# The reciprocal of softmax row sums, moved from VectorE to Newton steps on GpSimd

## The chip, the cores and the metric

The kernel runs on one core of a Trainium2 chip. The metric is the device time of one execution, in microseconds (us); lower is better. A core has five engines that work side by side: TensorE (PE in the profile) for matrix products, VectorE (DVE), ScalarE (ACT), GpSimd (POOL), and SyncE (SP), which here issues DMA transfers. Each engine runs its own instructions in program order. Where one needs the result of another, it waits on a semaphore.

## The reference: what is computed

Top-k attention with 8 batches, 8 heads, 576 positions and 64 values per head, then a feed-forward block on the 4608 rows of 512 values that it gives. All data is float32.

```python
scores = scale * np.matmul(q, k.transpose(0, 1, 3, 2))
kth = np.partition(scores, -top_k, axis=-1)[..., -top_k:-top_k + 1]   # top_k = 32
scores = np.where(scores >= kth, scores, -1000000000.0)
scores = scores - np.max(scores, axis=-1, keepdims=True)
attn = np.exp(scores)
attn = attn / (np.sum(attn, axis=-1, keepdims=True) + 1e-09)
x = np.matmul(attn, v)            # then heads side by side: 4608 x 512
h = x @ w_in                      # 512 -> 2048
g = h * np.cos(h)
out = g @ w_out                   # 2048 -> 512
```

The division in the sixth line is what the change concerns.

## The kernel before

The work is cut into 144 units. A unit is 128 query rows of one pair of heads, so most of its tiles have a middle dimension of 2. The main loop takes one slot per unit, and in a slot several units are in different stages: `u` searches its top 32, `w` (one slot older) is masked and exponentiated, `x` (two older) is normalised and its probabilities are split into 16-bit halves, `y` (three older) is transposed by a DMA, and `z` is a pair of units that are multiplied with the values. Pieces of the feed-forward block are put between.

VectorE searches: four rounds, each with a MAX8 and, but for the last, a MATCH_REPLACE8 for each of the two heads.

```python
def topk_round(u, rnd):
    ...
    for j in range(2):
        nc.vector.max(m8[:, j, at], src[:, j])                       # L237
    if rnd < TOPK // 8 - 1:
        for j in range(2):
            nc.vector.match_replace(rest[:, j], m8[:, j, at], src[:, j], NEG)   # L240
```

ScalarE masks and exponentiates, and sums each row as it does so. Then VectorE takes the reciprocal of the two sums of a row, and GpSimd multiplies:

```python
def exponentials(u):
    ...
    for j in range(2):
        nc.scalar.activation(out=s[:, j], in_=s[:, j], func=AF.Exp, bias=nd[:, j : j + 1],
                             scale=1.0, accum_out=den[:, j : j + 1])             # L268
    nc.scalar.activation(out=den, in_=den, func=AF.Identity, bias=eps, scale=1.0)  # L273

def reciprocal(u):
    u["rden"] = small.tile([P, 2], F32, tag="rden", name="rden")
    nc.vector.reciprocal(u["rden"], u.pop("den"))                                # L277

def normalise(u):
    s, rden = u["s"], u.pop("rden")
    for j in range(2):
        nc.gpsimd.tensor_scalar(out=s[:, j], in0=s[:, j], scalar1=rden[:, j : j + 1],
                                scalar2=1.0, op0=ALU.mult, op1=ALU.mult)         # L282

def split(u):
    ...
    halves = work.tile([P, 2, 2 * S], U16, tag="halves", name="halves", bufs=1)
    nc.gpsimd.tensor_copy(out=halves, in_=s.rearrange("p (k h) -> p h k", h=2))  # L294
```

`write_halves` then sends the halves to DRAM (`rows`), and `transposes` reads them back with a transposing DMA into `pT`, which TensorE multiplies with the values (L343).

GpSimd also works for the feed-forward block. For each tile `g` of 128 x 1024 hidden values it brings the argument of the cosine into range with four instructions (`reduce_first`, `reduce_second`), and after ScalarE's sine it multiplies (`gate`):

```python
gp.tensor_scalar(out=x, in0=g, scalar1=1.0, scalar2=0.25, op0=ALU.mult, op1=ALU.add)     # L431
gp.tensor_scalar(out=x, in0=x, scalar1=1.0, scalar2=MAGIC, op0=ALU.mult, op1=ALU.add)    # L432
gp.tensor_scalar(out=x, in0=x, scalar1=-MAGIC, scalar2=1.0, op0=ALU.add, op1=ALU.mult)   # L433
...
nc.gpsimd.tensor_tensor(out=x, in0=g, in1=x, op=ALU.subtract)                            # L440
...
eng.tensor_tensor(out=g, in0=g, in1=x, op=ALU.mult)                                      # L457, gate
```

Earlier still, while the weights arrive as 64-bit words, GpSimd has two more instructions for each weight piece (L147, L148). That is over after some 125 us.

The order of one slot of the main stage, cut to what matters (the other engines' calls stand between and run beside):

```python
def slot(i, u, w, x, y, z):
    if x: reciprocal(x)
    if u: topk_round(u, 0); ...
    if w: bounds(w); mask(w); exponentials(w)
    if u: topk_round(u, 1); topk_round(u, 2); topk_round(u, 3)
    ...                         # values(z), scores and take_scores of the next unit
    if y: transposes(y)
    gate(1)
    if x: normalise(x); split(x); write_halves(x)
    ...                         # feed-forward pieces
    reduce_first()
    reduce_second()
    ...
```

The first nine slots (`early_slot`) and the slots from the 142nd on (`last_slot`) transpose on TensorE instead (`transposes_now`). There the row sums, the reciprocal, the normalisation and the transposes of the same unit follow each other within one slot.

Of the kernel before, what the change touches and what calls it, by code (L numbers as in the profile page):

```python
# [10 lines left out]
F32 = mybir.dt.float32  # L11
I32 = mybir.dt.int32
U32 = mybir.dt.uint32
U16 = mybir.dt.uint16
AF = mybir.ActivationFunctionType
ALU = mybir.AluOpType

P = 128
# [7 lines left out]
INV_2PI = 1.0 / (2.0 * math.pi)  # L26
TWO_PI_BELOW = 6.283185005187988
MAGIC = 1.5 * 2.0**23


@with_exitstack
def kernel(
# [9 lines left out]
    nc = tc.nc  # L42
# [13 lines left out]
    consts = ctx.enter_context(tc.tile_pool(name="consts", bufs=1))  # L56
    loads = ctx.enter_context(tc.tile_pool(name="loads", bufs=5))
    work = ctx.enter_context(tc.tile_pool(name="work", bufs=2))
    small = ctx.enter_context(tc.tile_pool(name="small", bufs=4))
# [7 lines left out]
    nc.vector.memset(halfpi, math.pi / 2.0)  # L67
    eps = consts.tile([P, 1], F32, tag="eps")
    nc.vector.memset(eps, EPS)

# [191 lines left out]
    def exponentials(u):  # L264
        s, nd = u["s"], u.pop("nd")
        den = u["den"] = small.tile([P, 2], F32, tag="den", name="den")
        for j in range(2):
            nc.scalar.activation(  # L268
                out=s[:, j], in_=s[:, j], func=AF.Exp, bias=nd[:, j : j + 1], scale=1.0,
                accum_out=den[:, j : j + 1],  # L270
            )

        nc.scalar.activation(out=den, in_=den, func=AF.Identity, bias=eps, scale=1.0)  # L273

    def reciprocal(u):
        u["rden"] = small.tile([P, 2], F32, tag="rden", name="rden")
        nc.vector.reciprocal(u["rden"], u.pop("den"))  # L277

    def normalise(u):
        s, rden = u["s"], u.pop("rden")  # L280
        for j in range(2):
            nc.gpsimd.tensor_scalar(  # L282
                out=s[:, j], in0=s[:, j], scalar1=rden[:, j : j + 1], scalar2=1.0,
                op0=ALU.mult, op1=ALU.mult,
            )

# [127 lines left out]
    def reduce_first():  # L414
# [6 lines left out]
        if ff["end"]:  # L421

            nc.vector.tensor_scalar(
                out=x, in0=g, scalar1=0.25, scalar2=MAGIC, op0=ALU.add, op1=ALU.add
            )
            nc.vector.scalar_tensor_tensor(
                out=x, in0=x, scalar=MAGIC, in1=g, op0=ALU.subtract, op1=ALU.subtract
            )
            return
        gp = nc.gpsimd  # L430
# [4 lines that stand above are left out]
# [105 lines left out]
    def early_slot(i, u, w):  # L540
# [7 lines left out]
        if w:  # L548
            bounds(w)
            mask(w)  # L550
            exponentials(w)
            reciprocal(w)
# [5 lines left out]
        if w:  # L558
            normalise(w)
# [19 lines left out]
    def slot(i, u, w, x, y, z):  # L579
        if x:  # L580
            reciprocal(x)
# [3 lines left out]
        if w:  # L585
            bounds(w)
            mask(w)
            exponentials(w)
# [19 lines left out]
        if x:  # L608
            normalise(x)
            split(x)  # L610
            write_halves(x)
# [9 lines left out]
    def last_slot(i, u, w, x, y, z):  # L621
        if x:
            reciprocal(x)
# [3 lines left out]
        bounds(w)  # L627
        mask(w)
        exponentials(w)
        take_banks()  # L630
        sines(1)
# [10 lines left out]
        if x:  # L642
            normalise(x)
            split(x)
            write_halves(x)
# [25 lines left out]
    for i in range(NU + 1):  # L671
# [4 lines left out]
        u, w = (units[i - n] if 0 <= i - n < NU else None for n in range(2))  # L676
# [55 lines left out]
```

## Time and profile before

| | |
|---|---|
| median of three runs | 1535.46 us (1535.19 to 1535.78) |
| span of the profiled execution | 1530.3 us |
| reciprocal on VectorE (L277), 144 times | 22.9 us busy, 159 ns mean |
| VectorE waiting for the row sums before it | 17.4 us in 6 cases |
| GpSimd waiting for the reciprocal | 84.4 us in 29 cases |
| GpSimd waiting for the halves' DMA | 80.1 us in 42 cases |

A page of the profile is read from the top: the share of the span that each engine is busy, then the chain of work that ended last, followed back from the last instruction, then the costliest groups of instructions. A group's line names the source line, the engine, the operation, the tile written and the tiles read, the shapes and the count; after the first bar stand its busy time in us and the mean duration of one in ns, after the second the idle time of the engine just before these instructions and what ended most of it. Idle time of an engine that is not the bound costs nothing by itself, but it is the room in which that engine can take more work.

### The profile page before, as it was taken

The page shows a single profiled execution, that of the slowest core. Times are in us where ns is not written, and L with a number is a line of the kernel's source. Part 1 is how long each engine was busy: PE and PEld are TensorE (multiplying, and loading weights), DVE is VectorE, ACT ScalarE, POOL GpSimd, SP SyncE. Part 2 cuts the span into 40 slices and gives each one's busy share as a digit, 9 for nine tenths or more (in the row PEclk, how much of TensorE's full clock was granted, in tenths as well). Part 3 has the DMA queues.
Part 4 walks back from the last instruction along what each step waited for, and adds up shares of the span by engine and source line. Part 5 has one row for each costly group of instructions (what it writes and reads, how often), then busy time and mean ns, then how long its engine had stood idle before and what let it go on. Part 6 is the DMA issues. An engine that isn't in the chain of part 4 may idle for free.

```text
span 1530.3 us, 28322 instructions
## 1 busy us (share of the span) xinstructions
PE 1430.3 (93%) x10360; PEld 1022.7 (67%) x10360; DVE 1449.0 (95%) x3102; ACT 1109.6 (73%) x2150; POOL 1105.4 (72%) x838
## 2 busy tenths in 40 slices
PE   4678588999999999999999999999999999999998
PEld 3466266676767676767676767676767676767675
DVE  7999999999999999999999999999999999999911
ACT  7887667777777777777777777777777777777731
POOL 4778957777878787877777777777777778777600
PEclk6588899999999999999999999999999999999999
DMA  8432255645674556655565365645654446444200
GB/s 269 139 96 90 87 152 151 177 116 162 163 178 116 147 133 169 170 132 146 162 170 140 117 162 162 163 131 137 187 148 142 135 131 162 144 136 120 81 8 14
DMA packets 371740, 212.09 MB, mean 139 GB/s; under 512 B 321296, under 2 KB 337937, under 8 KB 371601
## 3 DMA queue, kind: packets, MB, share of 16 engines
q1 hardware_dynamic: 366192, 200.63, 48.4%
q10 hardware_dynamic: 5408, 9.65, 1.7%
q8 instruction: 81, 1.33, 0.4%
q14 instruction: 59, 0.48, 0.1%
HBM read 45.09 MB, written 87.29 MB: 87 GB/s over the span
## 4 chain that ended last, share of the span: by engine, by line
DVE 72%; PE 16%; ACT 5%; issue 5%; DMA 1%; POOL 0%; SPq 0%; ACTq 0%; POOLq 0%; DVEq 0%
DVE m L237 36%; DVE rest L240 33%; PE mm L393 6%; PE o L469 6%; PE o L343 2%; PE sc L213 1%; ACT s L268 1%; ACT s L260 1%; DVE w_out L138 1%; ACT st L127 1%; DVE rden L277 1%; DMA v<-in_v_dram 1%; ACT st L128 0%; PE tp L317 0%; DMA st<-in_moe_w_in_dram 0%
## 5 line engine op out<-in xcount | busy, mean ns | idle before, releaser
L393 PEld LDWEIGHTS mm<-xT,w_in 128*128 128x128 f32 x4608 | 546.6, 193 | 117.0 <-issue 95.2
L237 DVE MAX8 m<-rest 128x8 f32<-128x576 f32 x864 | 613.7, 757 | 0.0
L393 PE MATMUL mm<-xT,w_in 128*128 128x128 f32 x4608 | 567.0, 278 | 19.0 <-ACT xT L349 19.0
L469 PE MATMUL o<-w_out,g 128*128 128x512 f32 x1152 | 539.3, 600 | 11.5 <-POOL g L457 7.5
L240 DVE MATCH_REPLACE8 rest<-m,rest 128x576 f32<-128x576 f32 x576 | 426.4, 753 | 0.0
L469 PEld LDWEIGHTS o<-w_out,g 128*128 128x128 f32 x1152 | 202.7, 191 | 206.2 <-issue 190.7
L294 POOL COPY halves<-s 128x2304 uint16<-128x2304 uint16 x132 | 277.6, 2103 | 85.8 <-DMA rows<-halves 80.1
L282 POOL TENSOR_SCALAR s<-s,rden 128x576 f32<-128x576 f32 x288 | 212.3, 750 | 84.4 <-DVE rden L277 84.4
L268 ACT ACTIVATE s<-s,nd 128x576 f32<-128x576 f32 x288 | 219.5, 763 | 0.6
L240 DVE MATCH_REPLACE8 rest<-m,s 128x576 f32<-128x576 f32 x288 | 213.2, 753 | 0.0
L237 DVE MAX8 m<-s 128x8 f32<-128x576 f32 x288 | 203.1, 752 | 7.0 <-ACT s L223 7.0
L260 ACT ACTIVATE s<-s,nb 128x576 f32<-128x576 f32 x288 | 205.3, 760 | 0.0
L457 POOL TENSOR_TENSOR g<-g,x 128x1024 f32<-128x1024 f32 x68 | 161.4, 2374 | 57.3 <-ACT x L450 57.3
L213 PE MATMUL sc<-k,q 64*128 64x288 f32 (+1 forms) x1280 | 186.9, 439 | 14.5 <-ACT s L223 14.5
L223 ACT COPY s<-sc 128x1152 f32<-128x1152 f32 x144 | 160.6, 1115 | 39.9 <-PE sc L213 39.3
L343 PEld LDWEIGHTS o<-pT,v 128*64 128x64 f32 x2560 | 136.7, 141 | 69.2 <-issue 37.2
L343 PE MATMUL o<-pT,v 128*64 128x128 f32 (+1 forms) x2560 | 165.7, 272 | 14.3 <-ACT pT L321 8.4
L440 POOL TENSOR_TENSOR x<-g,x 128x1024 f32<-128x1024 f32 x68 | 161.3, 2372 | 5.7
L248 ACT ACTIVATE nb<-m 128x4 f32<-128x4 f32 x144 | 29.6, 206 | 185.3 <-DVE m L237 185.3
L405 ACT ACTIVATE g<-mm 128x512 f32<-128x512 f32 x144 | 84.3, 587 | 107.7 <-PE mm L393 107.7
L213 PEld LDWEIGHTS sc<-k,q 64*128 64x128 f32 (+1 forms) x1280 | 101.6, 182 | 66.5 <-ACT s L223 17.6
L431 POOL TENSOR_SCALAR x<-g 128x1024 f32<-128x1024 f32 x68 | 71.1, 1046 | 98.8 <-ACT g L405 94.0
(48 smaller groups left out, 1042.3 us busy)
## 6 DMA issues: line engine op xcount, KB each, us to landing
rows<-halves SPq DMA_DIRECT2D x132, 576.0 KB, 3.2
out_dram<-ob ACTq DMA_DIRECT2D x36, 256.0 KB, 2.1
q<-in_q_dram SPq DMA_DIRECT2D x31, 288.0 KB, 3.1
st<-in_moe_w_in_dram SPq DMA_DIRECT2D x16, 512.0 KB, 5.3
v<-in_v_dram SPq DMA_DIRECT2D x32, 256.0 KB, 3.5
st<-in_moe_w_out_dram SPq DMA_DIRECT2D x16, 512.0 KB, 3.6
k<-in_k_dram SPq DMA_DIRECT2D x31, 144.0 KB, 3.4
k<-in_k_dram SPq DMA_DIRECT2D x32, 128.0 KB, 3.9
```

Source lines behind the costliest of these rows:

```text
L213: nc.tensor.matmul(sc[r0 : r0 + rows, j, h, 0:HS], st["q"][d, q0 : q0 + rows], st["k"][d, h * HS : (h + 1) * HS], start=True, stop=True,)
L237: nc.vector.max(m8[:, j, at], src[:, j])
L240: nc.vector.match_replace(rest[:, j], m8[:, j, at], src[:, j], NEG)
L260: nc.scalar.activation(out=s[:, j], in_=s[:, j], func=AF.Prelu, bias=nb[:, j, 1:2], scale=SCALE, alpha=FAR)
L268: nc.scalar.activation(out=s[:, j], in_=s[:, j], func=AF.Exp, bias=nd[:, j : j + 1], scale=1.0, accum_out=den[:, j : j + 1],)
L282: nc.gpsimd.tensor_scalar(out=s[:, j], in0=s[:, j], scalar1=rden[:, j : j + 1], scalar2=1.0, op0=ALU.mult, op1=ALU.mult,)
L294: nc.gpsimd.tensor_copy(out=halves, in_=s.rearrange("p (k h) -> p h k", h=2))
L343: nc.tensor.matmul(o[d, to], lhsT, rhs, start=c == 0, stop=c == NT)
L393: nc.tensor.matmul(mm[:, at : at + w], w_in[f // FC][:, c, (f % FC) * P : (f % FC + 1) * P], blk["xT"][:, c], start=c == 0, stop=c == NC - 1,)
L440: nc.gpsimd.tensor_tensor(out=x, in0=g, in1=x, op=ALU.subtract)
L457: eng.tensor_tensor(out=g, in0=g, in1=x, op=ALU.mult)
L469: nc.tensor.matmul(o, g[:, at : at + P], w_out[f], start=f == 0, stop=f == NF - 1)
```

## The change

VectorE no longer computes the reciprocal. ScalarE makes a first guess by integer arithmetic on the bits of the row sum (a constant minus the bits, read as a float). GpSimd improves it with Newton's steps r' = r (2 - r d): two whole steps of three instructions each, and of a third step the factor e = 2 - r d with two instructions. The last product r e is not formed: the normalisation multiplies the row by r and by e, as its two scalars. So each unit has one instruction less on VectorE, one more on ScalarE and eight more on GpSimd, each of the eight on a tile of 128 x 2 and each reading what the one before it wrote. The purpose is to take work off VectorE.

```diff
+RECIP = float(0x7EF311C7)
...
+    recip = consts.tile([P, 1], F32, tag="recip")
+    nc.vector.memset(recip, RECIP)
...
         nc.scalar.activation(out=den, in_=den, func=AF.Identity, bias=eps, scale=1.0)
+        u["r"] = small.tile([P, 2], F32, tag="r0", name="r")
+        nc.scalar.activation(
+            out=u["r"].bitcast(I32), in_=den.bitcast(I32), func=AF.Identity, bias=recip, scale=-1.0
+        )
 
     def reciprocal(u):
-        u["rden"] = small.tile([P, 2], F32, tag="rden", name="rden")
-        nc.vector.reciprocal(u["rden"], u.pop("den"))
+        gp, den, r = nc.gpsimd, u.pop("den"), u.pop("r")
+        for n in range(3):
+            e = small.tile([P, 2], F32, tag=f"e{n}", name="e")
+            gp.tensor_tensor(out=e, in0=r, in1=den, op=ALU.mult)
+            gp.tensor_scalar(
+                out=e, in0=e, scalar1=-1.0, scalar2=2.0, op0=ALU.mult, op1=ALU.add
+            )
+            if n < 2:
+                to = small.tile([P, 2], F32, tag=f"r{n + 1}", name="r")
+                gp.tensor_tensor(out=to, in0=e, in1=r, op=ALU.mult)
+                r = to
+        u["rden"] = r, e
 
     def normalise(u):
-        s, rden = u["s"], u.pop("rden")
+        s, (r, e) = u["s"], u.pop("rden")
         for j in range(2):
             nc.gpsimd.tensor_scalar(
-                out=s[:, j], in0=s[:, j], scalar1=rden[:, j : j + 1], scalar2=1.0,
+                out=s[:, j], in0=s[:, j], scalar1=r[:, j : j + 1], scalar2=e[:, j : j + 1],
                 op0=ALU.mult, op1=ALU.mult,
             )
```

The calls of `reciprocal` and `normalise` stay where they are in every slot.

## The prediction

> **What bounds the kernel now.** I read the busy shares first, then the chain that ended last, then the middle of the run cut out as one stretch, then GpSimd's own groups and waits, because GpSimd is the engine that the change loads.
>
> The page's first part and the engine line of its chain:
>
> ```profile
> PE 1430.3 (93%) x10360; PEld 1022.7 (67%) x10360; DVE 1449.0 (95%) x3102; ACT 1109.6 (73%) x2150; POOL 1105.4 (72%) x838
> DVE 72%; PE 16%; ACT 5%; issue 5%; DMA 1%; POOL 0%; SPq 0%; ACTq 0%; POOLq 0%; DVEq 0%
> ```
>
> VectorE (DVE) is busy for 95% of the span and carries 72% of the chain; GpSimd (POOL) carries none of it. The answer by stretches, for the steady middle:
>
> ```profile
> core 0: us, PE busy (x) PEld busy (x) DVE busy (x) ACT busy (x) POOL busy (x), PEclk, DMA share, GB/s
> 200.00:1400.00 1200.00, 1177.22 (x8797) 844.37 (x8798) 1200.00 (x2599) 890.29 (x1726) 915.46 (x674) 0.99 0.55 149
> ```
>
> In these 1200 us VectorE has no gap. TensorE's busy time is 98%, so it stands close behind. 124 units of 128 query rows go through (the 124 copies of L294 below), so one slot lasts 1200/124 = 9.68 us. The chain of waits across the start of one slot:
>
> ```profile
> 711.26 0.07 DVE m L237
> 711.33 0.50 issue
> 711.83 0.76 DVE m L237
> 712.59 0.06 DVE rden L277
> 712.66 1.31 DVE m L237 x2
> ```
>
> The reciprocal is in that chain with 0.06 us, though its group has a mean of 159 ns: instructions on VectorE overlap, and only the step from one start to the next counts. Now GpSimd's groups in the same 1200 us (busy, mean ns, then the idle time before them and who ended it):
>
> ```profile
> L294 POOL COPY halves<-s 128x2304 uint16<-128x2304 uint16 x124 | 260.7, 2102 | 85.2 <-DMA rows<-halves 79.9
> L282 POOL TENSOR_SCALAR s<-s,rden 128x576 f32<-128x576 f32 x246 | 180.8, 747 | 39.3 <-DVE rden L277 39.3
> L440 POOL TENSOR_TENSOR x<-g,x 128x1024 f32<-128x1024 f32 x61 | 144.6, 2371 | 5.1
> L457 POOL TENSOR_TENSOR g<-g,x 128x1024 f32<-128x1024 f32 x60 | 142.2, 2370 | 48.9 <-ACT x L450 48.9
> L432 POOL TENSOR_SCALAR x<-x 128x1024 f32<-128x1024 f32 x61 | 63.8, 1046 | 5.3
> L431 POOL TENSOR_SCALAR x<-g 128x1024 f32<-128x1024 f32 x61 | 63.8, 1046 | 93.0 <-ACT g L405 88.2 <-ACT nb L248 4.8
> ```
>
> Its real waits are 79.9 + 39.3 + 48.9 + 88.2 + 4.8 = 261.1 us: 2.1 us of slack in each of the 124 slots. This is the room that the change has. How GpSimd spaces its instructions, from its timeline (start, duration, and in brackets the idle time before it):
>
> ```profile
> 702.32 1.05 POOL L431 TENSOR_SCALAR x<-g 128x1024 f32<-128x1024 f32 x1 [3.54 <-ACT g L405]
> 703.45 1.04 POOL L432 TENSOR_SCALAR x<-x 128x1024 f32<-128x1024 f32 x1
> ...
> 712.31 2.37 POOL L457 TENSOR_TENSOR g<-g,x 128x1024 f32<-128x1024 f32 x1 [0.60 <-ACT x L450]
> 714.65 1.48 POOL L282 TENSOR_SCALAR s<-s,rden 128x576 f32<-128x576 f32 x2
> ```
>
> L432 reads what L431 wrote: it starts 703.45 - 703.37 = 0.08 us after L431's end. L282 reads nothing of L457's and starts 0.03 us before L457 ends. A dependent step thus costs its duration and 0.08 us.
>
> **What the Trainium skill says.** (1) "GPSIMD Engine Reference", section "Instruction dispatch": consecutive GpSimd instructions are no barrier among its cores, so a reader of the previous result needs a wait on its completion. The trace agrees: 0.08 us of gap where there is a dependence, none where there is none. All eight new GpSimd instructions form one dependent chain. (2) The same page, section "Elementwise — side-by-side cycle accounting": every instruction passes two software dispatch hops, whatever its size, and an operation of two tensors costs about 2.6 cycles an element, one of a single tensor about 1. The trace agrees on the slope, 2.09 against 0.83 ns an element (worked out below), and shows a fixed part. (3) "ScalarE: Activation LUTs", section "What ACT_TABLE_LOAD costs": an ACTIVATE with a per-partition bias takes about 280 ns and 0.833 ns an element. The trace has 296 ns for the same form (the 128x2 Identity that adds eps). (4) "SBUF — State Buffer", section "Who interferes with whom": a VectorE instruction with one SBUF input outside the two-port modes doesn't contend with GpSimd. The trace agrees as far as it goes: MAX8 lies between 729 and 778 ns over the whole run, with GpSimd busy and idle by turns. So I give the new GpSimd work no cost on VectorE.
>
> **The change part by part, for one unit.**
>
> Removed from VectorE: one reciprocal, 0.06 to 0.07 us of chain. Over 124 slots 8 us, over 144 units 9 us. It also removes the places where VectorE stood still for ScalarE's row sums ("DVE rden L277 <- ACT den L273", 17.4 us in 6 cases). Four are in the first 92 us, 1.89 + 0.44 + 2.13 + 0.41 = 4.9 us, and those may be won; the other two (3.51 and 9.05 us) lie after 1436 us, where VectorE is no longer the bound.
>
> Added on ScalarE: one 128x2 Identity, 296 ns like its neighbour. With 890.3/1200 = 74% busy and waits of its own it can take this in the middle; it only matters where ScalarE is on the chain, at both ends.
>
> Added on GpSimd: five TENSOR_TENSOR and three TENSOR_SCALAR of 128x2. No instruction of that size and kind is in the trace, so I take the fixed part from two sizes of each kind. Two tensors: 1305 ns at 512 elements (the weight decode)
>
> ```profile
> L148 POOL TENSOR_TENSOR w_out<-w_out,st 128x512 f32<-128x512 f32 x16 | 20.9, 1305 | 1.3
> ```
>
> and 2371 ns at 1024: (2371 - 1305)/512 = 2.08 ns an element, fixed part 1305 - 1066 = 239 ns; with two elements 0.24 us. One tensor: 1046 ns at 1024 and 2102 ns at 2304 (the copy, another operation, so this is the looser fit): 1056/1280 = 0.825 ns, fixed part 201 ns; with two elements 0.20 us. With the gap of 0.08: 5 x 0.32 + 3 x 0.28 = 2.44 us.
>
> Changed on GpSimd: the normalisation has a second per-partition operand in place of a constant. By the one-tensor fit 576 elements should take 201 + 475 = 676 ns, and L282 takes 747: I put the 71 ns down to its one per-partition operand and expect up to as much again for the second, 2 x 0.07 = 0.14 us a unit. Between nothing and that I take 0.06. Sum on GpSimd: 2.5 us a unit.
>
> Now the balance in the middle. GpSimd needs 1200 - 261 (its waits) + 124 x 2.5 = 1249 us for what VectorE would do in 1200 - 8 = 1192. So the bound passes to GpSimd: 49 us longer, 10.07 us a slot. The point of balance is 1192 = 939 + 124 x A, A = 2.04 us a unit, or 0.255 us for each of the eight steps, gap included. My 2.5 is above it by a fifth.
>
> Units outside the window: 7 more belong to the middle stage, 7 x 0.4 = 3 us. In the nine early slots GpSimd had idle time of 2.4 to 5 us before most normalisations, so 2.4 us of new work about fits, and what VectorE saves there I let cancel against later transposes. In the last three slots the row sums, the reciprocal, the normalisation and the transposes follow each other directly; there the new chain adds 0.3 + 2.4 us and takes away 0.2 to 0.3, about 2.4 us each: 7 us, of which I count 5. Sum: 1535.5 + 49 + 3 + 5 = 1592 us.
>
> **The rivals.**
>
> (a) VectorE stays the bound and its removed time is won: 1535 - 9 - 5 + 5 = 1526 us, less only if TensorE, 98% busy, can follow. For it: VectorE's unbroken 1200 us. Against it: it needs steps under 0.255 us on GpSimd, where the gap alone is 0.08 and the two-tensor fixed part 0.24.
>
> (b) GpSimd is full only on average and the waits decide. Its work is in program order with the feed-forward's; late normalisations make the transposing DMA and then TensorE's values late, and TensorE has 2% of room. Some of the 261 us of waits would then remain. If a fifth of them stays, 50 us come on top: 1640 us. For it: the waits end on three different engines. Against it: most are waits of an engine that runs ahead, and they shrink when it falls behind; the wait on the DMA of the halves (79.9 us) should nearly vanish, since the new chain lies between two copies.
>
> (c) The small steps are cheaper than the fits say, 2.1 to 2.3 us a unit: 0 to 24 us in the middle, 1540 to 1567 us. For it: a 128x1 memset takes only 98 ns here. Against it: a memset reads nothing and waits for nothing.
>
> **Range and chances.** An error of 0.2 us in the sum of eight steps is 25 us. From 2.2 us (about 1555 us) to 2.8 us (1629 us), with (b) as the upper tail and (a) as the lower: 1550 to 1635 us. Faster by over 2% would need under 1505 us, more than everything that the change takes off VectorE: 0.02. Within 2% ends at 1566 us, which is A = 2.3 without friction: 0.20. Slower: 0.78.
>
> **What would show it right or wrong.** In the profile after: POOL's busy share up from 72% to 85 to 90%; eight POOL lines for `e` and `r` with 0.20 to 0.24 us each, started 0.28 to 0.32 us apart; VectorE's share below 95% and, in the middle, waits of MAX8 on ScalarE's copied scores or of VectorE behind TensorE that weren't there; the waits of POOL on the DMA of the halves nearly gone. The chain should go through POOL. It would be wrong if the steps lie under 0.25 us apart (then the time stays near 1535), or if POOL keeps large waits beside them (then it is over 1635).

## The result, and the profile after

The changed kernel takes 1632.8 us (median of four runs, 1629.2 to 1633.5) against 1535.4 us: a ratio of 1.063, 95% interval 1.061 to 1.065. It is slower by 97 us.

The first part of the page after, and the two lines of its chain, by engine and by source line (line numbers are those of the changed kernel: L240 and L243 search, L302 normalises, L314 splits, L451 to L460 bring the cosine's argument into range, L477 is the gate, L413 and L489 are the two products of the feed-forward block):

```profile
PE 1460.5 (90%) x10360; PEld 1037.2 (64%) x10360; DVE 1458.2 (90%) x2959; ACT 1154.5 (71%) x2294; POOL 1347.1 (83%) x1990
...
POOL 49%; PE 37%; issue 6%; ACT 5%; DMA 2%; SPq 0%; DVE 0%; POOLq 0%; ACTq 0%; DVEq 0%
PE mm L413 15%; PE o L489 14%; POOL halves L314 9%; POOL s L302 7%; POOL x L460 7%; POOL g L477 5%; PE sc L216 4%; PE o L363 3%; POOL e L290 3%; POOL x L453 3%; POOL x L452 3%; POOL e L289 3%; POOL x L451 3%; POOL r L295 2%; ACT s L271 1%
```

VectorE has gone from 72% of the chain to 0%, GpSimd from 0% to 49%, and TensorE (PE) from 16% to 37%. A GpSimd that is busy for 83% doesn't look full. GpSimd's groups between 200 and 1500 us show where the rest is:

```profile
L314 POOL COPY halves<-s 128x2304 uint16<-128x2304 uint16 x127 | 267.0, 2102 | 20.0 <-DMA rows<-halves 12.4
L302 POOL TENSOR_SCALAR s<-s,r,e 128x576 f32<-128x576 f32 x255 | 207.6, 821 | 6.8
...
L289 POOL TENSOR_TENSOR e<-r,den 128x2 f32<-128x2 f32 x381 | 74.3, 195 | 19.9
L290 POOL TENSOR_SCALAR e<-e 128x2 f32<-128x2 f32 x382 | 73.1, 191 | 34.1
...
L451 POOL TENSOR_SCALAR x<-g 128x1024 f32<-128x1024 f32 x62 | 64.8, 1045 | 28.8 <-ACT nb L251 28.8
L295 POOL TENSOR_TENSOR r<-e,r 128x2 f32<-128x2 f32 x254 | 49.5, 195 | 21.1
```

The small instructions have 19.9 + 34.1 + 21.1 = 75 us of idle time before them with nobody named as its cause: the gaps of the dependent chain. Such gaps aren't counted as busy, but GpSimd can't use them. Real waits, those with a name, come to about 43 us in these 1300, where before it was 261 in 1200. The wait for the halves' DMA has gone from 79.9 to 12.4 us. The chain itself in GpSimd's timeline, from its first instruction to the normalisation:

```profile
716.85 0.20 POOL L289 TENSOR_TENSOR e<-r,den 128x2 f32<-128x2 f32 x1
717.14 0.19 POOL L290 TENSOR_SCALAR e<-e 128x2 f32<-128x2 f32 x1
717.41 0.19 POOL L295 TENSOR_TENSOR r<-e,r 128x2 f32<-128x2 f32 x1
...
718.80 0.19 POOL L290 TENSOR_SCALAR e<-e 128x2 f32<-128x2 f32 x1
719.10 1.62 POOL L302 TENSOR_SCALAR s<-s,r,e 128x576 f32<-128x576 f32 x2
```

From the first start to the normalisation 2.25 us pass for eight steps: 0.28 us each, of which an instruction fills only 0.20. In about half of the slots a gate stands behind the chain; it doesn't read the chain's result and starts 2.11 us after the first step (756.77 to 758.88 us in the timeline).

**Where the 97 us lie.** The start of a unit's first MAX8 on VectorE is a clock for the whole pipeline. A slot is the mean distance of these starts from unit 16 to unit 140; the spans are those of the profiled executions. The four starts, units 16 and 140 of the kernel before, then of the changed one:

```profile
208.05 1.40 DVE L237 MAX8 m<-s 128x8 f32<-128x576 f32 x2
1411.09 1.42 DVE L237 MAX8 m<-s 128x8 f32<-128x576 f32 x2
223.01 1.41 DVE L240 MAX8 m<-s 128x8 f32<-128x576 f32 x2
1490.83 1.40 DVE L240 MAX8 m<-s 128x8 f32<-128x576 f32 x2
```

| | unit 16 starts | slot, units 16 to 140 | from unit 140's start to the end | span |
|---|---|---|---|---|
| before | 208.0 us | 9.702 us | 119.2 us | 1530.3 us |
| after | 223.0 | 10.224 | 136.6 | 1627.4 |
| difference | 15.0 | 124 x 0.522 = 64.7 | 17.4 | 97.1 |

So two thirds of the loss are in the steady middle and one third at the two ends. GpSimd's own demand in the middle, the time of a slot in which it waits for nobody, can be worked out for a stretch that all kernels spend in it, 250 to 1400 us: (1150 - named waits)/1150 x slot. The gaps of the chain count as demand. The named waits (us in total, times, longest) of the kernel before, then of the changed one:

```profile
POOL x L431 <- ACT g L405: 88.2, 42, 3.8
POOL halves L294 <- DMA rows<-halves: 74.2, 39, 5.1
POOL g L457 <- ACT x L450: 48.9, 28, 4.2
POOL s L282 <- DVE rden L277: 27.2, 14, 2.6
POOL x L431 <- ACT nb L248: 4.8, 1, 4.8
...
POOL x L451 <- ACT nb L251: 24.7, 14, 2.4
POOL halves L314 <- DMA rows<-halves: 5.5, 5, 1.9
POOL g L477 <- issue: 0.2, 1, 0.2
```

Before it is (1150 - 243.3)/1150 x 9.702 = 7.65 us, after (1150 - 30.4)/1150 x 10.224 = 9.95 us. The change added 2.30 us a unit. That explains a slot of 9.95 and leaves 0.27 to be explained: the 30.4 us in which GpSimd still waits.

### The profile page after: what moved, and what is told of

It is laid out like the page before. It is cut to its first block, busy times and chain, and to the rows that moved or that the text cites. A ratio compares the mean times of both kernels' runs of the same rounds, so it can differ in the third digit from the quotient of the medians.

```text
span 1627.4 us, 29358 instructions
## 1 busy us (share of the span) xinstructions
PE 1460.5 (90%) x10360; PEld 1037.2 (64%) x10360; DVE 1458.2 (90%) x2959; ACT 1154.5 (71%) x2294; POOL 1347.1 (83%) x1990
## 3 DMA queue, kind: packets, MB, share of 16 engines
q10 hardware_dynamic: 5408, 9.65, 1.6%
## 4 chain that ended last, share of the span: by engine, by line
POOL 49%; PE 37%; issue 6%; ACT 5%; DMA 2%; SPq 0%; DVE 0%; POOLq 0%; ACTq 0%; DVEq 0%
PE mm L413 15%; PE o L489 14%; POOL halves L314 9%; POOL s L302 7%; POOL x L460 7%; POOL g L477 5%; PE sc L216 4%; PE o L363 3%; POOL e L290 3%; POOL x L453 3%; POOL x L452 3%; POOL e L289 3%; POOL x L451 3%; POOL r L295 2%; ACT s L271 1%
## 5 line engine op out<-in xcount | busy, mean ns | idle before, releaser
L489 PE MATMUL o<-w_out,g 128*128 128x512 f32 x1152 | 563.6, 623 | 71.4 <-POOL g L477 60.1
L413 PEld LDWEIGHTS mm<-xT,w_in 128*128 128x128 f32 x4608 | 552.7, 195 | 106.0 <-issue 100.9
L240 DVE MAX8 m<-rest 128x8 f32<-128x576 f32 x864 | 609.5, 747 | 0.0
L413 PE MATMUL mm<-xT,w_in 128*128 128x128 f32 x4608 | 568.3, 280 | 4.7 <-ACT xT L369 4.7
L243 DVE MATCH_REPLACE8 rest<-m,rest 128x576 f32<-128x576 f32 x576 | 423.4, 743 | 0.0
L489 PEld LDWEIGHTS o<-w_out,g 128*128 128x128 f32 x1152 | 208.5, 197 | 276.5 <-issue 195.3
L314 POOL COPY halves<-s 128x2304 uint16<-128x2304 uint16 x132 | 277.6, 2103 | 20.3 <-DMA rows<-halves 12.4
L240 DVE MAX8 m<-s 128x8 f32<-128x576 f32 x288 | 202.9, 746 | 93.7 <-ACT s L226 93.7
L302 POOL TENSOR_SCALAR s<-s,r,e 128x576 f32<-128x576 f32 x288 | 235.0, 823 | 8.3
L243 DVE MATCH_REPLACE8 rest<-m,s 128x576 f32<-128x576 f32 x288 | 211.7, 743 | 0.0
L425 ACT ACTIVATE g<-mm 128x512 f32<-128x512 f32 x144 | 84.6, 589 | 169.4 <-PE mm L413 169.4
L460 POOL TENSOR_TENSOR x<-g,x 128x1024 f32<-128x1024 f32 x68 | 161.0, 2368 | 5.7
L477 POOL TENSOR_TENSOR g<-g,x 128x1024 f32<-128x1024 f32 x68 | 160.9, 2366 | 4.0 <-ACT x L470 3.9
L289 POOL TENSOR_TENSOR e<-r,den 128x2 f32<-128x2 f32 x432 | 85.1, 197 | 58.0 <-ACT r L278 35.4
L290 POOL TENSOR_SCALAR e<-e 128x2 f32<-128x2 f32 x432 | 82.9, 192 | 38.6
```

Of the source, the lines that this page charges most:

```text
L302: nc.gpsimd.tensor_scalar(out=s[:, j], in0=s[:, j], scalar1=r[:, j : j + 1], scalar2=e[:, j : j + 1], op0=ALU.mult, op1=ALU.mult,)
L413: nc.tensor.matmul(mm[:, at : at + w], w_in[f // FC][:, c, (f % FC) * P : (f % FC + 1) * P], blk["xT"][:, c], start=c == 0, stop=c == NC - 1,)
L489: nc.tensor.matmul(o, g[:, at : at + P], w_out[f], start=f == 0, stop=f == NF - 1)
```

## The experiments

Three theories stood at the start. Capacity: GpSimd's demand of 9.95 us a slot is over VectorE's 9.65, and this sets the pace. Order: the Newton chain stands ahead of the gate in GpSimd's queue and delays TensorE's second product, whatever the load. Ends: in the first and last slots the longer way from row sum to transposes is paid in full.

Four kernels went first. A time without an interval is that of one execution. The kernel before was run beside each group of experiments: 1532.2 us beside the first four, 1535.4 beside the second four, 1532.3 beside the last three. Differences of a few us between groups are therefore read from the slots and not from the times.

**after_gate**: the chain moves behind the gate.

```diff
     def slot(i, u, w, x, y, z):
-        if x:
-            reciprocal(x)
...
         gate(1)
         if x:
+            reciprocal(x)
             normalise(x)
```

> The changed kernel with the eight Newton instructions put behind the gate multiplication in GpSimd's queue of a main-stage slot instead of ahead of it; nothing left out. Capacity theory (GpSimd's 9.9 us of work per slot, against 7.6 before, sets the pace): the work is the same, so the slots stay near 10.2 us and the time between 1615 and 1640 us. Order theory (what costs is that the gate, and with it TensorE's second product, comes 2.2 us later): TensorE's 60 us of waiting for the gate vanishes and the time falls to 1560 to 1580 us.

Measured: 1600.3 us, between the two. The slot is 9.998 us. GpSimd's waits between 250 and 1400 us, all that there are:

```profile
POOL halves L314 <- DMA rows<-halves: 3.4, 3, 2.2
```

3.4 us in 1150: GpSimd works without a pause and the slot is its demand, (1150 - 3.4)/1150 x 9.998 = 9.97 us. The same work in the other order takes 10.224. Both theories hold, and can be told apart: capacity is worth 9.998 - 9.702 = 0.296 us a slot (37 us in 124 slots), the place ahead of the gate 0.226 us (28 us). TensorE's waits for the gate between 200 and 1480 us didn't vanish; they halved (the changed kernel, then this one):

```profile
PE o L489 <- POOL g L477: 60.1, 16, 8.0
PE o L489 <- POOL g L477: 28.8, 16, 5.9
```

So it isn't TensorE's wait by itself that costs, but whether GpSimd comes to a stop through it.

**five_ops**: one Newton step fewer, five small instructions instead of eight (a step of the computation is left out).

```diff
-        for n in range(3):
+        for n in range(2):
...
-            if n < 2:
+            if n < 1:
```

> The changed kernel with one Newton step fewer, so that five small GpSimd instructions are left per unit (the reciprocal is less exact; this part of the computation is left out). Capacity theory: the added GpSimd work falls from 2.33 to about 1.5 us per unit, GpSimd needs 9.1 us per slot, under VectorE's 9.63, and the middle goes back to VectorE's pace: slots of 9.65 to 9.8 us, 1535 to 1560 us in all with what the first and last slots still lose. Latency theory (each small instruction delays what comes after it, whoever is the bound): five eighths of the loss stay, about 1595 us.

Measured: 1542.6 us, a slot of 9.677 us. With three instructions fewer nothing is left of the loss in the middle (the slot is even 0.025 us under that of the kernel before), though the chain still stands ahead of the gate. The 10 us over the kernel before lie at the ends: unit 16 starts at 212.0 us, and 128.9 us follow unit 140's start. GpSimd's demand is (1150 - 55.4)/1150 x 9.677 = 9.21 us. The latency theory, which wanted 1595 us, falls for the middle: there GpSimd's delay costs when GpSimd is the bound.

**no_ops**: no Newton step; ScalarE's first guess goes into the normalisation by itself (Newton's steps are left out).

```diff
     def reciprocal(u):
-        gp, den, r = nc.gpsimd, u.pop("den"), u.pop("r")
-        for n in range(3):
-            ...
-        u["rden"] = r, e
+        u["rden"] = u.pop("r")
...
-scalar2=e[:, j : j + 1],
+scalar2=1.0,
```

> The changed kernel without any Newton instruction: the first guess from ScalarE goes into the normalisation by itself (Newton's steps are left out). It shows what taking the reciprocal off VectorE is worth when GpSimd pays nothing for it. Capacity theory: slots of 9.63 us, 9 us less in the main stage and up to 5 us in the early slots, 1520 to 1530 us. If the extra ScalarE instruction were a cost of its own, the time would be above 1540 us.

Measured: 1524.5 us against 1532.2 us, ratio 0.995 (0.994 to 0.997). The slot is 9.649 us, 0.053 us less than before. This is all that the change could win: 124 x 0.053 = 6.6 us in the middle. ScalarE's extra instruction costs nothing that shows. The stretch 250 to 1400 us of this run, by engine:

```profile
core 0: us, PE busy (x) PEld busy (x) DVE busy (x) ACT busy (x) POOL busy (x), PEclk, DMA share, GB/s
250.00:1400.00 1150.00, 1143.50 (x8530) 816.22 (x8528) 1149.22 (x2385) 900.52 (x1793) 891.59 (x658) 1.00 0.55 149
```

VectorE still has hardly a gap, and TensorE stands at 1143.5/1150 = 99.4%. From this it looks as if little more could have come from lighter work on VectorE; no run took more off it.

**newton_middle**: Newton's steps for units 8 to 139 alone; the first 8 and the last 4 keep VectorE's reciprocal.

```diff
+    def newton(u):
+        return 2 * NP <= u["n"] < NU - NP
...
     def reciprocal(u):
+        if not newton(u):
+            rd = small.tile([P, 2], F32, tag="rden", name="rden")
+            nc.vector.reciprocal(rd, u.pop("den"))
+            u["rden"] = rd, None
+            return
```

> The changed kernel with VectorE's reciprocal kept for the first 8 and the last 4 units and Newton's steps for the 132 between; nothing left out. If the first slots lost 15 us and the last ones 17 us to the longer chain from row sum to transposes, as the starts of the units in the trace say, the time falls by about 30 us to 1595 to 1605 us and the slots of the middle stay at 10.2 us. If those stages lose little (about 5 us, as the prediction had it), it stays at 1622 to 1630 us.

Measured: 1608.2 us, 25 us less than the changed kernel (21 by the spans), 3 us over what was expected. The slot stays at 10.237 us. Unit 16 starts at 211.4 us instead of 223.0, and the part after unit 140's start takes 125.6 us instead of 136.6. So the first slots account for 11.6 us and the last for 11.0. TensorE's waits for the normalised rows follow: 52.7 us up to unit 16 in the changed kernel, 34.3 here, 33.9 in the kernel before (the lines of the changed kernel and of the kernel before):

```profile
PE tp L337 <- POOL s L302: 52.7, 7, 12.6
PE tp L317 <- POOL s L282: 33.9, 7, 9.9
```

Part of the rest of those 15 us may be the weight decode (L148), which in the kernel before runs on GpSimd until some 176 us, not until 125: TensorE waits for it 11.2 us in the changed kernel, 6.5 here and 3.9 before.

The mechanism can be read in the timeline of the changed kernel, one of the last slots:

```profile
1541.84 0.29 ACT L276 ACTIVATE den<-den,eps 128x2 f32<-128x2 f32 x1
1542.16 0.29 ACT L278 ACTIVATE r<-den,recip 128x2 int32<-128x2 int32 x1
1542.53 0.20 POOL L289 TENSOR_TENSOR e<-r,den 128x2 f32<-128x2 f32 x1 [2.58 <-ACT r L278]
...
1544.77 1.64 POOL L302 TENSOR_SCALAR s<-s,r,e 128x576 f32<-128x576 f32 x2
```

From the start of the row sums' last instruction to the normalisation 2.93 us. In the kernel before it was 1439.91 - 1439.25 = 0.66 us at one of its last slots:

```profile
1439.25 0.29 ACT L273 ACTIVATE den<-den,eps 128x2 f32<-128x2 f32 x1
...
1439.91 1.47 POOL L282 TENSOR_SCALAR s<-s,rden 128x576 f32<-128x576 f32 x2 [5.33 <-DVE rden L277]
```

GpSimd waits here, and TensorE waits for it: the chain is latency, not load. 6.4 us of the last part's loss (125.6 against 119.2) stay with VectorE's reciprocal there; what holds them wasn't tried.

The next four test the capacity theory's slope, whether the parts add up, what a step consists of, and a way to have VectorE's share for less.

**eleven_after_gate**: one Newton step more, in the order of after_gate.

```diff
-        for n in range(3):
+        for n in range(4):
...
-            if n < 2:
+            if n < 3:
```

(The small results are kept in two tiles here, to save room.)

> The kernel of after_gate with one Newton step more, so that eleven small GpSimd instructions stand in each unit; nothing left out. Capacity theory: in after_gate GpSimd already had no waits left in the middle (3.4 us in 1150), so three more steps of 0.276 us lengthen every slot by 0.83 us, from 10.00 to 10.82 us, and the run to 1705 to 1725 us. If the slots of after_gate were held by something else (the table switches of ScalarE, TensorE), the slot grows by less than half of that and the run stays under 1660 us.

Measured: 1714.0 us, a slot of 10.766 us, 0.768 more than after_gate. Three steps of 0.276 us would be 0.83. GpSimd waits for 0.6 us in 1150. Once it is the bound, every step appended to GpSimd is paid almost in full, 144 times.

**middle_after_gate**: newton_middle and after_gate together.

> Both repairs of the order and of the ends together: VectorE's reciprocal for the first 8 and last 4 units, Newton behind the gate for the 132 between; nothing left out. If the three parts of the loss (GpSimd's capacity in the middle, the place ahead of the gate, the longer chains at the ends) add up, the run takes 1632 - 32 - 24 = 1576 us, within 6 us, with slots of 10.0 us: still 40 us over the kernel before, all of it GpSimd's capacity. If they hang together, it stays at 1590 us or more.

Measured: 1579.0 us, a slot of 10.014 us, unit 16 at 208.1 us as before the change. The parts add up: 3 us over what was expected. What is left, 44 us over the kernel before (1535.4 in these runs), is 124 x 0.31 = 39 us of GpSimd's capacity and some 8 us of the last slots (127.3 us after unit 140's start against 119.2), by the profiled executions.

**independent**: eight small instructions of the same kinds and sizes in the same place, but each reads only the row sum and the first guess (Newton's steps are left out; the last result stands in the place of Newton's factor).

```diff
-            e = small.tile([P, 2], F32, tag=f"e{n}", name="e")
-            gp.tensor_tensor(out=e, in0=r, in1=den, op=ALU.mult)
+            e = es[:, n]
+            if n in (1, 4, 7):
+                gp.tensor_scalar(out=e, in0=den, scalar1=-1.0, scalar2=2.0, op0=ALU.mult, op1=ALU.add)
+            else:
+                gp.tensor_tensor(out=e, in0=r, in1=den, op=ALU.mult)
```

> The changed kernel with eight small GpSimd instructions of the same kinds and sizes in the same place, but each reads only the row sum and the first guess and writes its own columns, so none waits for another (Newton's steps are left out: the factor used is not the right one). If the 0.08 us between two starts is the wait for the one before, the starts come 0.16 to 0.20 us apart, the added work falls from 2.3 to about 1.6 us and the run goes back to 1535 to 1560 us. If the small instructions start 0.28 us apart whatever they read, it stays at about 1630 us.

Measured: 1542.1 us, a slot of 9.676 us. In its timeline (the third line holds two instructions):

```profile
700.52 0.20 POOL L295 TENSOR_TENSOR es<-r,den 128x2 f32<-128x2 f32 x1
700.68 0.20 POOL L291 TENSOR_SCALAR es<-den 128x2 f32<-128x2 f32 x1
700.83 0.35 POOL L295 TENSOR_TENSOR es<-r,den 128x2 f32<-128x2 f32 x2
701.14 0.19 POOL L291 TENSOR_SCALAR es<-den 128x2 f32<-128x2 f32 x1
```

The instructions are as long as before, 0.20 us, but the starts are (701.14 - 700.52)/4 = 0.155 us apart instead of 0.28. Dependence costs 0.12 us in each step: 0.08 us of gap, and 0.04 us of overlap that is lost. From the first start to the normalisation, which still has to wait for the last step, it is 1.38 us (700.52 to 701.90) instead of 2.25: 0.87 us less. GpSimd's demand falls from 9.95 to 9.18 us, the difference between a GpSimd with room (59 us of named waits in 1150) and one that sets the pace.

**pow_one**: the kernel before, with the reciprocal as one GpSimd instruction, the row sum to the power of minus one. Nothing is left out.

```diff
-        nc.vector.reciprocal(u["rden"], u.pop("den"))
+        nc.gpsimd.tensor_tensor(out=u["rden"], in0=u.pop("den"), in1=minus, op=ALU.pow)
```

> The kernel before with the reciprocal as one GpSimd instruction, the row sums to the power of minus one (128x2), and nothing on VectorE or ScalarE for it; nothing left out. Capacity theory: GpSimd has about 2.0 us of room in a slot, so an instruction of up to 1.5 us is free there and VectorE's share is won: 1522 to 1532 us, the same as no_ops or a little over it at the ends. If a power takes GpSimd over 2 us for such a small tile, the run is longer than the kernel before.

Measured: 1527.7 us against 1535.4, ratio 0.995 (0.993 to 0.997). The slot is 9.640 us. The instruction in the view of its tile (shortest, median and longest in ns, then first and last start):

```profile
L279 POOL TENSOR_TENSOR rden<-den,minus x144: 691/706/1155, 27.0 to 1456.9; 128x2 f32<-128x2 f32 x144
```

0.706 us in the median: 3.6 of the small multiplications, but one instruction with one dependence in place of eight. GpSimd keeps 151 us of named waits in 1150.

Last, the 0.23 us of the place ahead of the gate, and whether pow_one's ends can be had more cheaply.

**later_ff2**: the changed kernel, with TensorE's second product further behind its gate in program order. The Newton chain stays ahead of the gate.

```diff
-        gated = sum(ff["tick"] >= t + 2 for t in blk["gated"])
+        gated = sum(ff["tick"] >= t + 4 for t in blk["gated"])
```

> The changed kernel with TensorE's second product put at least four feed steps behind its gate in program order instead of two (about one slot more of lead for GpSimd); the Newton chain stays ahead of the gate; nothing left out. If the 0.23 us per slot above GpSimd's own 9.95 us comes from TensorE standing still for a late gate and then feeding GpSimd late, the waits for the gate go and the slots fall to 9.95 to 10.05 us, 1595 to 1610 us in all (or a few us more, from second products left for the end). If the place ahead of the gate costs by something else, the slots stay at 10.2 us.

Measured: 1595.1 us, a slot of 9.964 us. In the changed kernel TensorE waited for the gate 60.1 us in 16 cases between 200 and 1480 us; here its matmuls don't at all. How that wait cost time can be followed in the changed kernel. TensorE stands still for the gate:

```profile
707.53 2.05 PE L413 MATMUL mm<-xT,w_in 128*128 128x128 f32 x16
713.15 3.20 PE L489 MATMUL o<-w_out,g 128*128 128x512 f32 x4 [3.57 <-POOL g L477]
```

and from there works without a wait until 744 us. It has lost more than these 3.57 us: the four matmuls take 3.20 us, where four of the same line take 1.88 at 723.31 us, and TensorE's granted clock from 713.1 to 716.4 us is 0.60. Then ScalarE waits for the first product, in its timeline:

```profile
744.38 0.60 ACT L425 ACTIVATE g<-mm 128x512 f32<-128x512 f32 x1 [2.51 <-PE mm L413]
```

and GpSimd waits for ScalarE, in GpSimd's:

```profile
745.06 1.04 POOL L451 TENSOR_SCALAR x<-g 128x1024 f32<-128x1024 f32 x1 [2.23 <-ACT nb L251]
```

The tile that L451 reads is written by the L425 that ends at 744.98; the profile names the later `nb` (L251), an instruction of the same engine. GpSimd, the bound, stands still because it delivered late itself one round earlier.

How much of its 2.23 us comes from the wait and how much from the lower clock, one round of newton_middle shows. There the chain stands ahead of the gate, too, and the same circle runs, every 80 to 82 us. Two rounds, a wait of TensorE's second product and GpSimd's wait some 30 us later (L501, L489 and L463 are here the second product, the gate and the first step of the range reduction):

```profile
949.38 1.98 PE L501 MATMUL o<-w_out,g 128*128 128x512 f32 x4 [3.39 <-POOL g L489]
979.49 1.05 POOL L463 TENSOR_SCALAR x<-g 128x1024 f32<-128x1024 f32 x1 [0.34 <-ACT nb L253]
...
1029.74 3.61 PE L501 MATMUL o<-w_out,g 128*128 128x512 f32 x4 [3.59 <-POOL g L489]
1061.59 1.05 POOL L463 TENSOR_SCALAR x<-g 128x1024 f32<-128x1024 f32 x1 [2.08 <-ACT nb L253]
```

TensorE stood still for about as long in both. But from 949.4 to 952.7 us its granted clock was 1.00, and from 1029.7 to 1033.0 us it was 0.50; GpSimd's wait is 0.34 us in the one and 2.08 in the other. By this single round most of the circle's loss is TensorE's lower clock behind the wait. No run changes the clock alone, so the share is not shown.

Move the chain behind the gate, or the product away from it, and the circle has slack: two different edits, the same slot of 9.96 to 10.00 us.

**pow_mix** and **pow_one_again**, run side by side: GpSimd's power for units 8 to 139 and VectorE's reciprocal for the others, and pow_one once more.

```diff
+        if 2 * NP <= u["n"] < NU - NP:
             nc.gpsimd.tensor_tensor(out=u["rden"], in0=u.pop("den"), in1=minus, op=ALU.pow)
+        else:
+            nc.vector.reciprocal(u["rden"], u.pop("den"))
```

> The reciprocal as one GpSimd power in the middle (units 8 to 139) and on VectorE for the first 8 and last 4 units; nothing left out. The middle should stay at 9.64 us a slot and the end lose the 4 us that pow_one's last slots take more than the kernel before: 1521 to 1527 us, clear of the kernel before and level with pow_one or 1 to 4 us under it. If the early slots gain more from VectorE's freedom than the ends lose, it is over pow_one's 1527.7 us.

> The kernel of pow_one once more, in the same rounds as pow_mix, so that the two can be told apart: 1525 to 1530 us.

Measured: pow_mix 1525.9 us (1525.5 to 1526.3), pow_one 1528.7 us (1527.4 to 1531.8), the kernel before 1532.3 us (1530.5 to 1535.0). The ratios to the kernel before are 0.996 (0.995 to 0.997) and 0.998 (0.997 to 0.999). The gain of pow_one is 3.6 us here, where it was 7.7 in its first group; the kernel before itself differs by 3 us between the two. Both slots are 9.644 us; after unit 140's start pow_mix takes 120.1 us and pow_one 123.4. pow_mix is the best version found that computes all of the reference, some 0.4% under the kernel before and 6.5% under the changed one.

| kernel | small GpSimd instructions, place | slot | us |
|---|---|---|---|
| before | none | 9.702 | 1535.4 |
| no_ops | none | 9.649 | 1524.5 |
| pow_mix | 1 (power), middle only | 9.644 | 1525.9 |
| pow_one | 1 (power) | 9.640, again 9.644 | 1527.7, again 1528.7 |
| independent | 8, not dependent | 9.676 | 1542.1 |
| five_ops | 5, ahead of the gate | 9.677 | 1542.6 |
| middle_after_gate | 8, behind, middle only | 10.014 | 1579.0 |
| later_ff2 | 8, ahead, later product | 9.964 | 1595.1 |
| after_gate | 8, behind | 9.998 | 1600.3 |
| newton_middle | 8, ahead, middle only | 10.237 | 1608.2 |
| after | 8, ahead | 10.224 | 1632.8 |
| eleven_after_gate | 11, behind | 10.766 | 1714.0 |

The times stand beside 1532.2 to 1535.4 us of the kernel before. The slots fall into two groups with nothing between: up to a GpSimd demand of 9.2 us they are VectorE's 9.64 to 9.68 (9.70 in the kernel before, where VectorE still has the reciprocal), and from 9.93 on they are GpSimd's demand, with some 0.25 us on top in the changed kernel and newton_middle, where the gate waits behind the chain and the second product is near.

## Why the prediction was right or wrong

**The mechanism was right.** The bound passes from VectorE to GpSimd, through eight dependent small instructions, and VectorE's 0.06 us a slot can't pay for them. five_ops, independent and pow_one lie under the point of balance and keep VectorE's pace; after_gate and eleven_after_gate lie above it and follow GpSimd's demand. Rival (a), VectorE stays the bound, fell. What it named as removed was too much as well: no_ops shows 8 us, where 9 + 5 were named, and the 5 for the early slots didn't come. That the new work costs VectorE nothing held: between 250 and 1400 us MAX8 and MATCH_REPLACE8 are no longer than before (747 and 743 ns against 759 and 755).

**The steps were sized a little too large.** I took 239 and 201 ns for the fixed parts; the small instructions last 195 and 191 ns. The gap of 0.08 us was right. The chain came to 2.25 us ahead of a normalisation and 2.11 ahead of a gate, less 0.04 by which it overlaps what stands in front of it, instead of 2.44. The second per-partition operand was worth what the fit gave (71 ns estimated, 821 - 747 = 74 measured), 0.15 us a unit, of which I had counted only 0.06. The sum by GpSimd's demand is 2.30 us against 2.5.

**The middle without friction** would be at 9.96 to 10.00 us a slot (later_ff2, after_gate), against the predicted 10.07: 37 us instead of 49 over its 124 slots.

**The friction was the term that was missing.** Rival (b) had it, as waits that remain beside a full GpSimd, at up to a fifth of 261 us; the sum of 1592 us had nothing for it. It is 28 us. I had named the transposing DMA as its way, but in the changed kernel it runs through the gate: GpSimd late, TensorE's second product late, ScalarE's copy late, GpSimd idle. TensorE has little room (2% in the view of before), so what it loses by the wait of 3.6 us and by the lower clock behind it isn't made up 30 us later. The prediction had no step for that clock. The wait on the halves' DMA vanished as expected.

**The ends were mis-sized.** I let the early slots cancel and counted 5 us for the last, and 3 for 7 more units of the middle stage. Up to unit 16 the loss is 15 us, after unit 140 it is 17. newton_middle ties 11.6 and 11.0 us of this to the Newton chain at the ends. For the early slots I had compared GpSimd's idle time with its new work, as if it were a matter of load. There it is one of latency: TensorE's wait for the normalised rows in the first 223 us rose to 52.7 us from 33.9. VectorE's 4.9 us of waits for the row sums did go, and bought nothing: in no_ops, too, unit 9 starts at 126.5 us, as before at 126.1.

So 1592 us would have been 1580 us with the right step, and the 28 us of friction and some 24 us more at the ends (32 in place of 5 + 3) bring it to 1632. The measured 1632.8 us lies inside the range, close to its upper end, and that is in part luck. The upper end stood for steps of 2.8 us a unit (1629 us), with rival (b) beyond it; the steps were 2.3, and what filled the gap was a friction by another way, and ends of four times the size counted.

**The signs** came out as named but for one. VectorE's busy share fell to 90%, MAX8 waits 62.4 us for the copied scores between 250 and 1400 us, where it had not waited before, the steps start 0.28 us apart, and the wait for the halves' DMA is 12.4 us. But GpSimd's busy share, forecast at 85 to 90%, is 83%: the gaps of the chain, which the sum had, don't count as busy.

## What to carry to other kernels

Before moving work to an engine with idle time, work out that engine's demand per slot, gaps of dependent instructions included, and its point of balance; a busy share of 72% left room for 2.0 us a slot here, and eight dependent instructions on two numbers a row took 2.3. A chain of tiny dependent instructions is paid by the piece, not by the element, so one slower instruction (a power of 0.71 us) can beat eight fast ones. And when an in-order engine comes near its limit, put the result that another nearly full engine waits for ahead of the new work, or start its reader later.

## What the runs showed that I had not expected

A TENSOR_TENSOR with a power on 128x2 numbers takes GpSimd 0.706 us, against 0.195 us for a multiplication. Independent small instructions on GpSimd start 0.155 us apart with durations of 0.20 us, so they overlap; dependent ones take 0.28 us. And a straight line through 512 and 1024 elements overstates the fixed part of a two-tensor instruction: 239 ns by the line, 195 ns at two elements.
